# Splitting the last partitions of wo's tail into two small loads, and a section entry signalled by GpSimd

## The chip, the cores and the metric

The kernel runs on one core of a Trainium2 chip. The metric is the device time of one execution in microseconds (us); lower is better. Each time is a median of several runs; beside them one execution was taken by the profiler.

## The reference

A decode step mixes two branches by a gate. Branch A is attention over a cache (4 batches, 32 heads, 4096 keys of 128 floats); branch B is a feed-forward block with a gated GELU. All is float32.

```python
q = (x @ wq)                        # x: 4 x 1 x 512, wq: 512 x 4096, then 32 heads of 128
scores = einsum("bhqd,bhkd->bhqk", q, k_cache) * 128 ** -0.5
o = einsum("bhqk,bhkd->bhqd", softmax(scores), v_cache)
a = o.reshape(B, Sq, H * Dh) @ wo   # wo: 4096 x 512
b = (gelu(x @ w_gate) * (x @ w_up)) @ w_down
g = sigmoid((x * gate_w).sum(-1))
out = g * a + (1 - g) * b
```

The two caches are 268 MB each (4 x 32 x 4096 x 128 floats); wq and wo have 8.4 MB each and the three matrices of branch B 3.7 MB each. Each byte is read once.

## The kernel before, in words

The kernel is written as a list of steps. Each step names its engine, what it reads and what it writes, and a small planner (`Plan`) works out the waits: every lane (an engine, or a named lane for loads) has a semaphore, and a step waits for the lanes whose earlier steps it depends on. All loads are issued by SyncE (SP) through one helper, `load` (L251), and so stand in one queue in the order in which they are issued.

The work goes through 32 turns, one for each group of four heads and each batch. In a turn the keys of four heads come as one load of 8.4 MB (128 partitions x 16,384 floats), VectorE multiplies them by the query and sums (L377, L383), softmax follows on VectorE and ScalarE, and TensorE multiplies the weights with the values, another load of 8.4 MB (L409). All this works in one SBUF tensor, `big`, in which places are given out by hand.

Ahead of the turns stands an opening: the loads of wq, x, the first keys and the gate's weights. They are issued inside a critical section (`tc.tile_critical`, L585), whose entry and exit are signalled by one engine, by default SP. The other engines wait for its exit at a barrier (L588).

Behind the last turn come the loads of w_down (`load_d`) and of wo in two halves (`load_w`, L272). Half 0 comes in two loads. Half 1 comes in six: its 16 rows of 512 floats a partition are cut at 0, 4, 8, 11, 13 and 15, and each piece has a lane of its own, in this order f0, f1, g, v, y, w. The rows have `e` as their number; `DM` is 512, `P` is 128 and `E` is 16. For each row `e` of half 1, `project` (L478) makes four matmuls into `acc` from 32 columns of the attention's result and the row; `attended` (L469) says which places it reads, so a row waits for the lane that its piece came by. Row 15 is the last to come. Then VectorE copies `acc` to `res` (L578), and SP stores it (L579). At the end GpSimd clears the semaphores.

```python
    WO_END = ((0, E // 2, E), (0, 4, 8, 11, 13, 15, E))
```

Of the kernel before, what the change touches and what calls it, by code (L numbers as in the profile page):

```python
# [132 lines left out]
def tile_gated_mix(tc: tile.TileContext, x, kc, vc, wq, wo, w_gate, w_up, w_down, gate_w, out):  # L133
    nc = tc.nc
    P = 128
    B, H, S, D = kc.shape
    DM = x.shape[2]
# [15 lines left out]
    E = HW * D // P  # L153
# [12 lines left out]
    def sb(pool, name, shape):  # L166
        sizes[name] = math.prod(shape[1:])
        return pool(name, [P] + list(shape[1:]), F32).ap()[:shape[0]]
# [35 lines left out]
    q = sb(ps, "q", [P, B, D])  # L204
# [7 lines left out]
    W1, ES = TW, TW + TW // 2  # L212
    XS, U0, QD, FU, FT, OXA = VA - 2 * DM, VA - 4 * DM, VA - DM, VA + 2 * KC * F, ES + 2 * E * 32, ES + 2 * E * 32 + DM

    def place(a, n):
        return big[:, a:a + n]

    def z(a, n):
        return ("big", a, a + n)
# [4 lines left out]
    xTf = xT.rearrange("p c j b k -> p c (j b k)")  # L224
    selv = sel.rearrange("p j t m -> p j (t m)")
    x_sb = place(XS, DM)[:B]
    u = place(U0, 2 * DM).rearrange("p (s n) -> p s n", s=2)
    qd = place(QD, D)
    fu = place(FU, 2 * DM).rearrange("p (s n) -> p s n", s=2)
    OX = place(OXA, E * GW * HT * D // E)[:B * HT].rearrange("q (e g h k) -> q e g h k", e=E, g=GW, h=HT)  # L230
# [19 lines left out]
    def load(dst, src, writes, lane):  # L250
        return add("sp", lambda: nc.sync.dma_start(dst, src), (), writes, lane=lane, unit=16)  # L251
# [20 lines left out]
    def load_w(w):  # L272
        src = wo[w * HW * D:(w + 1) * HW * D].rearrange("(p e) n -> p (e n)", e=E)
        for n, (e0, e1) in enumerate(zip(WO_END[w], WO_END[w][1:])):
            a, m = (W0, W1)[w] + e0 * DM, (e1 - e0) * DM
            load(place(a, m), src[:, e0 * DM:e1 * DM], [z(a, m)], (("q", "x"), ("f0", "f1", "g", "v", "y", "w"))[w][n])

    load(place(Q0, KC * H * D), wq.rearrange("(p c) n -> p (c n)", c=KC), [z(Q0, KC * H * D)], "q")
    load(x_sb, x.rearrange("b s d -> (b s) d"), [z(XS, DM)], "x")
# [188 lines left out]

    def attended(w, e):  # L469
        a, m = ES + w * E * 32 + e * 32, (W0, W1)[w] + e * DM  # L470
        return place(a, 32), place(m, DM), [z(a, 32), z(m, DM)]

    def project_wide(s, w, reads):
        n = next(wide_rest)
# [49 lines left out]
    for i in range(NT):  # L524
        g, b = divmod(i, B)
# [30 lines left out]
    plan.turn = None  # L556
    load_d()
    load_w(0)
    load_w(1)
    expand(0)  # L560
    pv(NT - 1)
# [11 lines left out]
    for e in range(E):  # L573
        project_wide(*attended(0, e))
    fold()
    for e in range(E):
        project(*attended(1, e), False, e == E - 1)
# [4 lines left out]
        assert lane in ("sp", "out") or plan.knew[plan.steps[-1]][lane] == len(row_) - 1, lane  # L582
    plan.close()
    issued = nc.alloc_semaphore("issued")
    with tc.tile_critical(no_gpsimd_drain=True):  # L585
        plan.play(plan.steps[:opening])
    tc.close()
    tc.compile()  # L588
# [32 lines left out]
```

## Time and profile before

| What | Value |
|---|---|
| time, median of 3 runs | 1309.91 us (1309.84 to 1310.15) |
| time of the profiled execution | 1309.79 us |
| its span, first to last instruction | 1308.5 us |
| HBM read | 564.67 MB, 432 GB/s over the span |
| VectorE busy | 1153.3 us (88%) |
| TensorE matmul busy | 357.9 us (27%) |
| ScalarE busy | 86.9 us (7%) |
| GpSimd busy | 0.7 us |
| granted TensorE clock, mean | 0.636 |

The time is a little longer than the span, which runs from the first to the last instruction. The busy shares are means over the whole span. DMA engines aren't among the engines of the table; the profile gives their busy share as a mean over the core's 16.

### The profile page before, as it was taken

How to read it: one execution, taken by the hardware profiler on the slowest of the kernel's cores; microseconds unless marked ns; L12 is line 12 of the kernel's file. 1: busy time of each engine (PE TensorE's matmuls, PEld its weight loads, DVE VectorE, ACT ScalarE, POOL GpSimd, SP SyncE). 2: the span in 40 equal slices, each digit the busy share in tenths (PEclk: the TensorE clock that was granted, in tenths of full speed). 3: DMA queues.
4: the chain of work that ended last, by engine and by line, in shares of the span. 5: the costliest groups of instructions: out<-in, count | busy, mean ns of one | idle time of the engine just before them, and what ended most of it. 6: DMA issues, size and time to landing. Idle time of an engine off the chain costs nothing.

```text
span 1308.5 us, 6298 instructions
## 1 busy us (share of the span) xinstructions
PE 357.9 (27%) x2584; PEld 104.8 (8%) x2584; DVE 1153.3 (88%) x295; ACT 86.9 (7%) x289; POOL 0.7 (0%) x6
## 2 busy tenths in 40 slices
PE   2402333212332211322321123321123222122327
PEld 0200001000010000100000000100001000000003
DVE  1899999999899998989989898998989899898991
ACT  0000000000000000000000000000000000000001
POOL 0000000000000000000000000000000000000000
PEclk9656666556676656666655666655566665666668
DMA  9999999999999999999999999999999999999998
GB/s 417 417 447 427 437 439 427 439 431 441 425 441 425 443 427 439 439 429 439 431 441 425 441 425 443 427 439 439 429 441 429 441 425 441 425 443 429 435 431 364
DMA packets 11126, 564.82 MB, mean 432 GB/s; under 512 B 1368, under 2 KB 1384, under 8 KB 1900
## 3 DMA queue, kind: packets, MB, share of 16 engines
q1 hardware_dynamic: 11116, 564.68, 99.7%
q8 instruction: 7, 0.11, 0.0%
q14 instruction: 3, 0.02, 0.0%
HBM read 564.67 MB, written 0.01 MB: 432 GB/s over the span
## 4 chain that ended last, share of the span: by engine, by line
DMA 72%; DVE 26%; PE 1%; issue 1%; SPq 0%; ACT 0%; DVEq 0%
DMA big<-in_A_k_cache 66%; DVE sc L383 13%; DVE big L377 12%; DMA big<-in_A_wo 2%; DMA big<-in_B_w_up 2%; DMA big<-in_A_x 2%; PE po L312 1%; PE q L494 0%; SPq L251 0%; PE acc L481 0%; DVE hT L513 0%; DVE xT L303 0%; DVE m L388 0%; DVE big L511 0%; DVE big L508 0%
## 5 line engine op out<-in xcount | busy, mean ns | idle before, releaser
L377 DVE TENSOR_TENSOR big<-big,qb 128x4096 f32<-128x4096 f32 x64 | 556.0, 8687 | 87.7 <-DMA big<-in_A_k_cache 87.7
L383 DVE TENSOR_REDUCE sc<-big 128x32 f32<-128x4096 f32 x64 | 555.9, 8686 | 2.3
L409 PE MATMUL po<-big,PM 128*32 128x512 f32 x2048 | 296.1, 743 | 899.6 <-DMA big<-in_A_v_cache 899.6
L409 PEld LDWEIGHTS po<-big,PM 128*32 128x32 f32 x2048 | 72.7, 133 | 1116.6 <-DMA big<-in_A_v_cache 824.0
L395 ACT ACTIVATE PM<-sc,nb 32x128 f32<-32x128 f32 x128 | 67.2, 525 | 476.7 <-DVE nb L390 429.7
L417 ACT ACTIVATE o<-po 128x512 f32<-128x512 f32 x16 | 9.6, 597 | 449.8 <-PE po L409 449.8
L395 ACT ACTIVATION_READ_ACCUMULATOR PM<-sc,nb 32x1 f32 x128 | 26.1, 204 | 0.0
L367 ACT ACTIVATE qb<-q 128x512 f32<-128x512 f32 x8 | 4.8, 597 | 246.0 <-PE q L365 246.0
L426 PE MATMUL sm<-o,sel 128*16 128x128 f32 x128 | 15.4, 273 | 5.1 <-ACT o L417 5.1
L303 DVE COPY xT<-sg 128x128 f32<-128x128 f32 x4 | 0.9, 283 | 17.1 <-PE sg L298 17.1
L459 DVE TENSOR_TENSOR tm<-oT,gmask 128x256 f32<-128x256 f32 x2 | 0.8, 424 | 16.2 <-PE oT L453 16.2
L494 PE MATMUL q<-big,xT 128*32 128x448 f32 x64 | 10.5, 823 | 9.5 <-DMA big<-in_B_w_gate 4.9
L426 PEld LDWEIGHTS sm<-o,sel 128*16 128x16 f32 x128 | 11.7, 97 | 12.8 <-ACT o L417 11.4
L365 PE MATMUL q<-QM,hc 128*128 128x512 f32 x16 | 9.5, 678 | 4.2 <-DVE hc L361 4.2
L388 DVE TENSOR_REDUCE m<-sc 128x1 f32<-128x128 f32 x32 | 9.2, 286 | 1.1
L578 DVE COPY res<-acc 128x128 f32<-128x128 f32 x1 | 0.3, 291 | 10.1 <-PE acc L481 10.1
L312 PE MATMUL po<-big,xT 128*32 128x512 f32 x64 | 8.5, 692 | 1.0 <-DVE xT L303 1.0
L389 DVE STREAM_TRANSPOSE mt<-m 128x32 f32<-128x32 f32 x32 | 6.8, 211 | 1.1
L329 DVE TENSOR_TENSOR big<-po,amask 128x512 f32<-128x512 f32 x2 | 1.3, 686 | 7.3 <-PE po L312 7.3
L390 DVE TENSOR_REDUCE nb<-mt 128x1 f32<-128x32 f32 x32 | 6.0, 186 | 1.1
L298 PE MATMUL sg<-ident,big 4*128 4x4 f32 x4 | 0.6, 254 | 23.0 <-DMA big<-in_A_x 23.0
L481 PE MATMUL acc<-big 128*32 128x128 f32 x128 | 4.6, 276 | 1.8 <-DMA big<-in_A_wo 1.8
(62 smaller groups left out, 62.9 us busy)
## 6 DMA issues: line engine op xcount, KB each, us to landing
big<-in_A_wo SPq DMA_DIRECT2D x2, 2048.0 KB, 22.9
big<-in_B_w_gate SPq DMA_DIRECT2D x1, 3584.0 KB, 17.7
big<-in_B_w_up SPq DMA_DIRECT2D x1, 3584.0 KB, 26.9
big<-in_B_w_down SPq DMA_DIRECT2D x1, 3584.0 KB, 18.4
big<-in_A_wo SPq DMA_DIRECT2D x2, 1024.0 KB, 25.6
big<-in_A_wo SPq DMA_DIRECT2D x2, 512.0 KB, 29.2
big<-in_A_wo SPq DMA_DIRECT2D x1, 768.0 KB, 28.0
big<-in_A_k_cache SPq DMA_DIRECT2D x32, 29.7
```

The lines of the kernel that those rows point to most:

```text
L312: last = T.matmul(PO[s][32 * j:32 * j + 32].rearrange("p j d -> p (j d)"), xTf[:, c, :32], w[:, n0:n0 + HB * D], start=c == 0, stop=c == K ...
L365: pe(lambda: T.matmul(q.rearrange("p b d -> p (b d)"), HC.rearrange("p h k -> p (h k)"), QM.rearrange("p b d -> p (b d)"), start=True, sto ...
L377: dve(lambda: V.tensor_tensor(k, k, QB[:, b:b + 1, :].to_broadcast([P, r1 - r0, D]), op=OP.mult), m + t("qb"), m)
L383: dve(lambda: V.tensor_reduce(SC[i % 2][:, r0:r1], k, axis=AX.X, op=OP.add), [z(KA(i) + r0 * D, (r1 - r0) * D)], [(f"sc{i % 2}", r0, r1)])
L388: dve(lambda: V.tensor_reduce(M1[n], SC[n], axis=AX.X, op=OP.max), t(f"sc{n}"), t(f"m1{n}"))
L389: dve(lambda: V.transpose(MT, M1[n].to_broadcast([P, PH])), t(f"m1{n}"), t("mt"))
L390: dve(lambda: V.tensor_reduce(NB[n], MT, axis=AX.X, op=OP.max, negate=True), t("mt"), t(f"nb{n}"))
L395: last = A.activation(PM[:, PZ:].rearrange("p (c m) -> p c m", m=32)[s, :, h:RJ * HT:HT], SC[n][s, :].rearrange("p (c j) -> p c j", j=RJ), ...
L409: last = T.matmul(PO[n][32 * c:32 * c + 32].rearrange("p j d -> p (j d)"), PM[:, m0:m0 + 32], place(VAT(i) + j * N, N), start=b == 0 and j ...
L417: act(lambda: A.activation(O[n], PO[n], AF.Copy), t(f"po{n}"), t(f"o{n}"))
L426: T.matmul(sm[:B * HT, :D], selv[:, j, m0:m0 + B * HT], O[n][:, j, :], start=(n, j) == (0, 0), stop=(n, j) == (N - 1, RJ - 1))
L494: last = T.matmul(q.rearrange("p b d -> p (b d)")[32 * j:32 * j + 32, :FG], xTf[:, c, :32], place((F0, F1)[s] + c * F + j * FG, FG), start ...
```

## The change

There are two parts. First, for rows 11 to 15 of wo's half 1 (the loads v, y and w), the loads take only partitions 0 to 111. Partitions 112 to 127 of these five rows come in two loads of eight partitions each, with 2,560 floats (10,240 B) a partition, issued ahead of v, on new lanes e and h. Rows 11 to 15 read these places too, so TensorE waits for both ahead of row 11. Second, the critical section of the opening is entered and left on GpSimd's signal instead of SP's: SP loses an instruction that signals and keeps the wait, and GpSimd gets them.

```diff
+    UP = 11
...
         for n, (e0, e1) in enumerate(zip(WO_END[w], WO_END[w][1:])):
             a, m = (W0, W1)[w] + e0 * DM, (e1 - e0) * DM
-            load(place(a, m), src[:, e0 * DM:e1 * DM], [z(a, m)], (("q", "x"), ("f0", "f1", "g", "v", "y", "w"))[w][n])
+            if (w, e0) == (1, UP):
+                for p, lane in ((112, "e"), (120, "h")):
+                    load(place(a, (E - UP) * DM)[p:p + 8], src[p:p + 8, UP * DM:], [("upper", p, p + 8)], lane)
+            p = 112 if w == 1 and e0 >= UP else P
+            load(place(a, m)[:p], src[:p, e0 * DM:e1 * DM], [z(a, m)], (("q", "x"), ("f0", "f1", "g", "v", "y", "w"))[w][n])
...
-        return place(a, 32), place(m, DM), [z(a, 32), z(m, DM)]
+        return place(a, 32), place(m, DM), [z(a, 32), z(m, DM)] + ([("upper", 112, P)] if w == 1 and e >= UP else [])
...
-    with tc.tile_critical(no_gpsimd_drain=True):
+    with tc.tile_critical(sync_engine=mybir.EngineType.Pool, no_gpsimd_drain=True):
         plan.play(plan.steps[:opening])
```

## The prediction

> **What bounds the kernel now.** I read the page first, then the DMA share over long stretches, then the chain of waits and the timeline at the two ends.
>
> ```profile
> span 1308.5 us, 6298 instructions
> q1 hardware_dynamic: 11116, 564.68, 99.7%
> q8 instruction: 7, 0.11, 0.0%
> q14 instruction: 3, 0.02, 0.0%
> DMA 72%; DVE 26%; PE 1%; issue 1%; SPq 0%; ACT 0%; DVEq 0%
> ```
> ```profile
> 60.00:600.00 540.00, 133.74 (x924) 36.17 (x924) 501.60 (x121) 36.03 (x123) 0.00 (x0) 0.62 1.00 435
> 600.00:1264.00 664.00, 175.16 (x1200) 48.10 (x1204) 610.16 (x132) 43.58 (x149) 0.00 (x0) 0.62 1.00 434
> ```
>
> The second fence is the table by stage; its last two columns are the DMA share and GB/s. From 60 to 1264 us the sixteen DMA engines are busy for all of the time at 435 GB/s. The chain's 26% for DVE is therefore an accident of how it is followed (a load's issue waits for DVE), since the queue behind that issue never runs dry. The kernel is a stream of 564.68 MB. Its end can move in only three ways: the stream's first packet starts at another time, its last bytes land at another time, or the work behind the last landing changes. The change touches the first two. The price of a byte on one engine is 435/16 = 27.2 GB/s, so a row of 10,240 B (five of wo's rows of 512 floats) takes 0.38 us, one of 4,096 B 0.15 us, one of 2,048 B 0.075 us.
>
> The end, by the chain of waits and then by the timeline:
>
> ```profile
> 1275.61 29.56 DMA big<-in_A_wo
> 1305.21 1.06 PE acc L481 x24
> 1306.30 0.29 DVE res L578
> ```
> ```profile
> 1302.69 0.86 PE L481 MATMUL acc<-big 128*32 128x128 f32 x24 [0.76 <-DMA big<-in_A_wo]
> 1303.97 0.64 PE L481 MATMUL acc<-big 128*32 128x128 f32 x16 [0.42 <-DMA big<-in_A_wo]
> 1305.21 1.02 PE L481 MATMUL acc<-big 128*32 128x128 f32 x24 [0.60 <-DMA big<-in_A_wo]
> 1305.81 0.16 PEld L481 LDWEIGHTS acc<-big 128*32 128x32 f32 x8 [0.22 <-DMA big<-in_A_wo]
> 1306.62 0.67 SPq L579 DMA_DIRECT2D out<-res  x1
> ```
>
> PE starts at 1303.97 on rows 11 and 12 (the load named v), at 1305.21 on rows 13 and 14 (y), and at 1305.81 on row 15 (w). The 24 matmuls from 1305.21 take 1.02 us, although 24 in a row take 0.86 (the first line), because the last eight wait for w. So w's landing sets the end, and 1305.81 + 0.42 is the end of PE. The y landing has 1305.81 + 0.42 - (1305.21 + 0.86) = 0.16 us of slack.
>
> When does w land, and why so late? The table by stage again, near the end:
>
> ```profile
> 1303.00:1303.75 0.75, 0.56 (x22) 0.28 (x12) 0.00 (x0) 0.00 (x0) 0.00 (x0) 1.00 1.03 402
> 1303.75:1304.00 0.25, 0.03 (x4) 0.03 (x5) 0.00 (x0) 0.00 (x0) 0.00 (x0) 1.00 0.63 254
> 1304.00:1304.25 0.25, 0.25 (x12) 0.25 (x16) 0.00 (x0) 0.00 (x0) 0.00 (x0) 1.00 0.60 238
> 1304.25:1304.50 0.25, 0.25 (x16) 0.10 (x4) 0.00 (x0) 0.00 (x0) 0.00 (x0) 1.00 0.41 164
> 1304.50:1304.75 0.25, 0.12 (x5) 0.00 (x0) 0.00 (x0) 0.00 (x0) 0.00 (x0) 1.00 0.42 164
> 1304.75:1305.00 0.25, 0.00 (x0) 0.00 (x0) 0.00 (x0) 0.00 (x0) 0.00 (x0) 1.00 0.40 156
> 1305.00:1305.25 0.25, 0.04 (x4) 0.04 (x6) 0.00 (x0) 0.00 (x0) 0.00 (x0) 1.00 0.26 98
> 1305.25:1305.50 0.25, 0.25 (x12) 0.25 (x16) 0.00 (x0) 0.00 (x0) 0.00 (x0) 1.00 0.05 16
> ```
>
> Multiply the share by 16: all engines work until 1303.75, then 10, 10, 7, 7, 6, 4 and 1. Every engine carries the same bytes, yet about six stop before 1304, about three more before 1304.5, and about six go on to 1305.0-1305.4. What the engines do not share evenly is the ten instruction packets of q8 and q14 (first fence): seven of 0.11 / 7 = 0.016 MB, three of 0.02 / 3, some half of that. One of them, by the DMA view of 1292.5 to 1292.7 us:
>
> ```profile
> q8 instruction: 1, 0.02, 27.7%
> ```
>
> 0.277 x 16 x 0.2 us = 0.89 us on one engine. The stream never pauses, so what such a packet takes is never won back. My reading: the late six each met one q8 packet, the three in the middle one q14 packet. Work moved from the late engines to the early ones brings the end forward; the unused area above is (0.37 + 0.40 + 0.59 + 0.58 + 0.60 + 0.74 + 0.95) x 0.25 x 16 = 17 engine-us, so at most 17/16 = 1.06 us is there to gain.
>
> **The loads of rows 11 to 15.** Before, each engine carries 8 partitions of the three loads v, y, w. After, these have 112 partitions, 7 an engine if sixteen still share them evenly, and partitions 112 to 127 come in two loads of eight rows of 10,240 B, issued ahead of v. How does a load of few rows spread? The x load has four rows of 2,048 B and lands in four partitions. Two windows of 30 ns show its packets:
>
> ```profile
> DMA packets 5, 0.01 MB, mean 205 GB/s; under 512 B 2, under 2 KB 2, under 8 KB 5
> q1 hardware_dynamic: 5, 0.01, 56.2%
> DMA packets 3, 0.00 MB, mean 69 GB/s; under 512 B 2, under 2 KB 2, under 8 KB 3
> ```
>
> Three packets of 2 to 8 KB start within 30 ns, and one 0.17 us later. 0.562 x 16 x 30 = 270 ns of packet time for the three and two tiny ones, so some 85 ns each: they overlap, so they are on different engines, one row each, and lie in neighbouring partitions without slowing one another. So I take a load of eight rows as one row on each of eight engines, both loads on the same eight, call these the low eight, and the others the high eight. The Trainium skill (DMA: Bandwidth & Descriptors, section "Why a DMA increments its semaphore by 16 and not by 1") says that the number of engines is the largest one up to 16 that divides the rows, and that on the queues of SP the lowest-numbered are used; which eight, no view of before shows.
>
> Against before, at w's landing: a high engine has one row less, -0.38 us; a low engine has two more and one less, +0.38. At y's landing: high -2 x 0.15 = -0.30, low 0.76 - 0.30 = +0.46. At v: high -0.15, low +0.61.
>
> If the six late engines are all high, w's last landing goes from 1305.81 to 1305.43 for PE. The latest low engine is then one that stops at 1304.75 or so before and at 1305.13 after, against 1305.4 - 0.38 = 1305.0 for the high: the two sides end about together, and I allow 0.1 us there. For y PE starts at 1304.91 and would be done with 24 matmuls at 1305.77; w gives 1305.43 + 0.42 = 1305.85 and still sets the end. **-0.38 us.** Where the late engines lie can't be read before, and I take the high eight: the two classes of lateness go by queue (six by q8, three by q14), no engine shows two, so these packets have fixed homes, and a queue with its homes in one half is the simplest such pattern. That is a choice, not a reading.
>
> PE gets two more waits ahead of row 11, for the two small loads. They stand ahead of v in the same queue, and PE sat idle 0.42 us before 1303.97 on v alone, then 0.60 before 1305.21: that hides them, and even v's +0.61 on the early engines only fills what they had to spare. SP issues two loads more:
>
> ```profile
> 1275.13 0.43 SPq L251
> big<-in_A_wo SPq DMA_DIRECT2D x1, 256.0 KB, 29.7
> ```
>
> Two times 0.43 us delays w's issue by 0.9, and behind these on SP is only the output, at 1306.62. The w load lands 29.7 us after its issue, so a queue of nearly 29 us covers it; without that cover it would cost 0.9. Sixteen packets more, at 0.01 us of gaps each pair: nothing.
>
> **The entry.** The chain of waits at the start:
>
> ```profile
> 0.67 0.05 issue
> 0.72 0.02 SPq L585
> 0.74 0.07 issue
> 0.80 0.03 SPq L588
> 0.84 0.12 issue
> 0.96 0.40 SPq L251
> 1.42 21.40 DMA big<-in_A_x
> ```
> ```profile
> 0.34 0.10 POOL L610 MEMSET const-uint8-127<- 128x1 uint8 x1
> ```
>
> SP now signals to itself (L585) and then waits for it (L588), from 0.72 to 0.80; then comes the first load. After, GpSimd signals and SP only waits. GpSimd is done with its memsets at 0.44 and leaves the opening barrier about when SP does. If its signal is there when SP arrives, the load starts 0.08 us earlier; if it lags by a signal's flight, the gain is none or below: bounds +0.05 (half an issue gap of 0.12) and -0.08, and I take -0.06, nearer the row that goes away. The whole stream shifts with it. At the section's exit GpSimd's signal reaches the engines perhaps 0.1 us later; SP's next load waits for PE's projection and PE for x, which lands at 1.42 + 21.40, so nothing follows from it.
>
> **Sum.** The profiled execution took 1309.79 us (1308.5 of span and 1.29 around it); the median of the runs is 0.12 above it. 1309.79 - 0.38 - 0.06 = 1309.35, in terms of the median 1309.5 us: 0.03% faster, far inside the 0.2% (2.6 us) that a measurement of this kernel can tell from no change.
>
> **The rivals.**
> - *The late engines carry the small loads.* If the last engine of all is one of the low eight, its end moves by +0.38: PE starts row 15 at 1306.19, and the time is 1309.91 + 0.38 - 0.06 = 1310.2, slower than before. It decides as soon as the very last engine is low; if only an earlier one of the six is low (they stop 0.1 to 0.4 before the last), the end moves by 0 to +0.3, and the time lies between 1309.9 and 1310.2. For it: no view places them. Chance 0.26.
> - *The change doesn't do what it says.* If the small loads spread over all sixteen, or one on each half, every engine carries 8 rows as before, and only the entry is left: 1309.85. The packets of x speak against the first, nothing against the second. Chance 0.10. [...]
> - *An instruction packet more.* SP's program grows by two loads and the fetches shift; one more q8 packet on a late engine costs some 0.9 us: 1310.4 at best, with the gain of 0.38 taken off. Ten in 1308 us speak against it. Chance 0.06.
> - *112 partitions go slower than 128.* If seven rows an engine, no longer in step with eight partitions, took twice as long, that is 7 x 0.38 = 2.7 us more: 1312.1. The neighbours of the x load speak against it. Chance 0.02.
>
> **How the numbers follow.** The forecast has 0.55, the four rivals 0.44, and 0.01 is left for what I don't see. Forecast and first two rivals span 1309.35 to 1310.2; with the entry's bounds and the 0.3 us between the runs of before the range is 1309.2 to 1310.3. Faster than 1307.3 nothing here reaches (the whole unused area is 1.06 us): 0.01. Slower than 1312.5: the last rival's worst, 0.02. Within: 0.97.
>
> **What would show it.** Right: in the timeline SP's first load starts near 0.90; the share of DMA falls from full to nothing in a shorter stretch than the 1.75 us of before; PE starts row 15 about 0.38 earlier relative to the first load. Wrong: the staircase is as long or longer, with its last engines later (first rival), unchanged (second), or the landings of v, y, w are spaced wider than 1.24 and 0.60 us for every engine (fourth). A time outside 1309.2 to 1310.3 would say that something moved which is not in this list.

## The result, and the profile after

The changed kernel takes 1313.31 us (median of 11 runs, 1312.69 to 1313.67) against 1309.90 before: a ratio of 1.0024, 95% interval 1.0016 to 1.0033. It is slower by 3.4 us, where 0.4 us faster was forecast. Its profiled execution took 1313.05 us.

The start, by the chain of waits of the changed kernel (start, us, what):

```profile
0.61 0.02 POOLq L616
0.63 0.06 issue
0.69 0.02 POOLq L591
0.72 0.02 issue
0.73 0.03 SPq L594
0.77 0.12 issue
0.89 0.41 SPq L253
```

GpSimd signals at 0.69 and SP stops waiting at 0.73; the first load is issued at 0.89 in place of 0.96. That is the -0.07 which was forecast as -0.06.

The end, by the timeline of TensorE (PE):

```profile
1300.72 1.08 PE L487 MATMUL acc<-big 128*32 128x128 f32 x32 [0.28 <-DMA big<-in_A_wo]
1304.37 0.86 PE L487 MATMUL acc<-big 128*32 128x128 f32 x24 [2.57 <-DMA big<-in_A_wo]
1307.14 2.36 PE L487 MATMUL acc<-big 128*32 128x128 f32 x40 [1.90 <-DMA big<-in_A_wo]
1307.98 1.07 PEld L487 LDWEIGHTS acc<-big 128*32 128x32 f32 x24 [0.21 <-DMA big<-in_A_wo]
```

Rows 4 to 7 (the 32 matmuls) start at 1300.72, a tenth earlier than before. From there on all is late: row 8 starts at 1304.37 in place of 1302.69, row 11 at 1307.14 in place of 1303.97, row 13 at 1307.98 in place of 1305.21. SP's issues did not delay it: by the DMA view the load w (224 KB) landed 31.8 us after its issue, and the last issue of wo's ends at 1277.9. Why the bytes came late stands in the table by stage (the last three columns are PE's granted clock, DMA share and GB/s; a packet counts in full where it starts, so a share can pass 1), first before, then after:

```profile
1300.00:1302.00 2.00, 1.93 (x68) 1.45 (x56) 0.00 (x0) 0.00 (x0) 0.00 (x0) 1.00 1.02 422
1302.00:1304.00 2.00, 0.89 (x28) 0.62 (x29) 0.00 (x0) 0.00 (x0) 0.00 (x0) 1.00 0.95 382
1306.00:1306.50 0.50, 0.23 (x8) 0.00 (x0) 0.20 (x1) 0.00 (x0) 0.00 (x0) 1.00 0.00 0
```
```profile
1300.50:1301.00 0.50, 0.28 (x12) 0.28 (x16) 0.00 (x0) 0.00 (x0) 0.00 (x0) 1.00 1.41 438
1301.00:1301.50 0.50, 0.50 (x28) 0.50 (x20) 0.00 (x0) 0.00 (x0) 0.00 (x0) 1.00 0.92 160
1302.00:1304.00 2.00, 0.00 (x0) 0.00 (x0) 0.00 (x0) 0.00 (x0) 0.00 (x0) 1.00 0.99 223
1305.00:1306.00 1.00, 0.23 (x11) 0.00 (x0) 0.00 (x0) 0.00 (x0) 0.00 (x0) 1.00 0.95 250
1307.00:1307.50 0.50, 0.36 (x8) 0.39 (x12) 0.00 (x0) 0.00 (x0) 0.00 (x0) 0.50 0.29 111
1308.00:1308.50 0.50, 0.50 (x17) 0.49 (x16) 0.00 (x0) 0.00 (x0) 0.00 (x0) 0.50 0.00 0
```

All engines stay busy (0.99, 0.95) but move half the bytes: 223 to 250 GB/s instead of 382 to 422. The fall is sudden, from 438 to 160 GB/s at 1301, when the small loads and the first load of 112 partitions are under way (the 438 counts in full the rows of 10,240 B that start there). Single packets show the same: a row of the load g (6,144 B, one of 128 partitions) takes 0.234 us up to 1300, and from 1301 to 1303.5 every one of them takes 0.40 to 0.61. Had the loads piled up on a few engines, these would be busy and the others idle; here every engine is busy and slow.

The table shows a second loss. PE's granted clock is 0.50 from 1307 on, where before it was 1.00 until PE was done. The 24 matmuls from 1307.98 end with PE at 1309.50 (1307.14 + 2.36): 1.52 us, against 0.86 at full clock. At full clock w, landing at 1308.46, would have ended them at 1308.46 + 0.04 + 0.42 = 1308.92. So of the 3.27 us by which PE ends later (1306.23, that is 1305.21 + 1.02, to 1309.50), 0.58 are the clock and 2.69 the late landing, with the entry's gain already taken off.

### The profile page after: what moved, and what is told of

Read it like the earlier page. It is cut to its first block, busy times and chain, and to the rows that moved or that the text cites. A ratio compares the mean times of both kernels' runs of the same rounds, so it can differ in the third digit from the quotient of the medians.

```text
span 1311.7 us, 6303 instructions
## 1 busy us (share of the span) xinstructions
PE 356.3 (27%) x2584; PEld 105.7 (8%) x2584; DVE 1153.3 (88%) x295; ACT 86.9 (7%) x289; POOL 0.7 (0%) x6
## 3 DMA queue, kind: packets, MB, share of 16 engines
q1 hardware_dynamic: 11100, 564.68, 99.6%
## 4 chain that ended last, share of the span: by engine, by line
DMA 72%; DVE 26%; PE 1%; issue 1%; SPq 0%; ACT 0%; DVEq 0%; POOLq 0%
DMA big<-in_A_k_cache 66%; DVE sc L389 13%; DVE big L383 12%; DMA big<-in_A_wo 2%; DMA big<-in_B_w_up 2%; DMA big<-in_A_x 2%; PE po L318 1%; PE q L500 0%; PE acc L487 0%; SPq L253 0%; DVE hT L519 0%; DVE m L394 0%; DVE xT L309 0%; DVE big L517 0%; DVE big L516 0%
## 5 line engine op out<-in xcount | busy, mean ns | idle before, releaser
L415 PE MATMUL po<-big,PM 128*32 128x512 f32 x2048 | 292.9, 736 | 902.8 <-DMA big<-in_A_v_cache 902.8
```

What stands on the lines that cost most here:

```text
L415: last = T.matmul(PO[n][32 * c:32 * c + 32].rearrange("p j d -> p (j d)"), PM[:, m0:m0 + 32], place(VAT(i) + j * N, N), start=b == 0 and j ...
```

## Experiments: which part

Each time is a median beside the kernel before on the same chip, which took 1309.82 to 1309.88 us throughout.

**Entry only.**

```diff
-    with tc.tile_critical(no_gpsimd_drain=True):
+    with tc.tile_critical(sync_engine=mybir.EngineType.Pool, no_gpsimd_drain=True):
```

> Only the entry is signalled by GpSimd; the loads are as before. My step says -0.06 us: 1309.85, and SP's first load at 0.89 us of the span, as it stands after the whole change. If the entry carried part of the loss, the time would be above 1310.5.

Measured: 1309.96 us, ratio 1.000 (0.999 to 1.001). Its chain starts as that of the changed kernel does (first load at 0.89), so the 0.07 us are there at the start and too small for the runs to show. The entry carries none of the loss.

**Split loads only**, the changed kernel with the old entry.

> Only the loads of rows 11 to 15 are split; SP signals the entry. If the loads carry the whole loss: 1313.4 (0.07 above the whole change). First rival (only more bytes on late engines, at the usual price): at most 1310.3.

Measured: 1313.43 us, ratio 1.0027 (1.0017 to 1.0036). The loads carry all of it, and far above the 1310.3 that more bytes on late engines could give at the usual price.

**Small loads only.**

```diff
+            if (w, e0) == (1, 11):
+                for p, lane in ((112, "e"), (120, "h")):
+                    for a2, m2, c0 in ((VA + TW - 2 * DM, 2 * DM, 11 * DM), (VA - DM, DM, 13 * DM)):
+                        load(place(a2, m2)[p:p + 8], src[p:p + 8, c0:c0 + m2], ..., lane)
             load(place(a, m), src[:, e0 * DM:e1 * DM], [z(a, m)], ...)
```

> The loads v, y, w keep 128 partitions; ahead of v stand four loads of eight rows (partitions 112 to 119 and 120 to 127, 4,096 B and 2,048 B a row) into places that nothing reads, 12 KB more on each of eight engines. At the usual price 12,288 B / 27.2 = 0.45 us: 1310.4 at most. If the small loads are what slows all engines: 1 us more or above, 1311 to 1312, and the lines of the load g stretched as in the changed kernel.

Measured: 1311.23 us, ratio 1.001 (1.000 to 1.002): +1.35, three times the price of its bytes. In its trace w lands 1.2 us later than before (1306.97 for 1305.77); the rest is PE's half clock. The table by stage:

```profile
1300.00:1301.00 1.00, 0.28 (x12) 0.28 (x16) 0.00 (x0) 0.00 (x0) 0.00 (x0) 1.00 0.97 395
1301.00:1302.00 1.00, 0.81 (x32) 0.54 (x20) 0.00 (x0) 0.00 (x0) 0.00 (x0) 1.00 1.09 295
1302.00:1303.00 1.00, 0.00 (x0) 0.00 (x0) 0.00 (x0) 0.00 (x0) 0.00 (x0) 1.00 0.97 270
1303.00:1304.00 1.00, 0.37 (x16) 0.38 (x19) 0.00 (x0) 0.00 (x0) 0.00 (x0) 1.00 1.02 373
```

The rate falls while the small loads run (270) and comes back behind them (373), with v, y and w at 128 partitions. From 1301 to 1303 all 28 rows of g take 0.29 to 0.53 us in place of 0.234, so the small loads slow every engine that still carries g.

**112 partitions only.**

```diff
-            load(place(a, m), src[:, e0 * DM:e1 * DM], [z(a, m)], ...)
+            p = 112 if w == 1 and e0 >= 11 else P
+            load(place(a, m)[:p], src[:p, e0 * DM:e1 * DM], [z(a, m)], ...)
```

> The loads v, y, w take 112 partitions and the small loads are left out, so partitions 112 to 127 of rows 11 to 15 hold old values. At the usual price one row less an engine: -0.38 us, 1309.5. If loads of 112 partitions are what slows the engines (240 GB/s, as seen in the changed kernel, in place of 435): 1.15 MB take 4.8 us in place of 3.0 for 128 partitions, +1.8 and some 0.5 more at the end if TensorE's clock falls before its last matmuls: 1311.7 to 1312.2.

Measured: 1311.88 us, ratio 1.0016 (1.0007 to 1.0026): +2.0, although an eighth of the bytes of these rows isn't moved.

```profile
1300.00:1301.00 1.00, 0.06 (x4) 0.00 (x0) 0.00 (x0) 0.00 (x0) 0.00 (x0) 1.00 1.02 424
1302.00:1303.00 1.00, 0.08 (x4) 0.00 (x0) 0.00 (x0) 0.00 (x0) 0.00 (x0) 1.00 1.08 236
1303.00:1304.00 1.00, 0.00 (x0) 0.00 (x0) 0.00 (x0) 0.00 (x0) 0.00 (x0) 1.00 1.00 240
```

236 and 240 GB/s with busy engines, as in the changed kernel. Both parts slow the stream by themselves: 1.35 + 2.0 = 3.35, against 3.55 together. (The sum is rough, as the half clock lies in each.)

## Experiments: reads or writes

No view shows which engine writes which partition. I assumed that an engine takes neighbouring rows of a load: with 128 partitions eight rows of wo into eight neighbouring partitions, with 112 seven, so that most eights would be shared by two engines; in the small loads eight engines would share one. But row and partition have the same number, so the collision could be in HBM (theory S) or in SBUF (theory D). Four kernels pair them in all ways. All of half 1 comes in pairs of loads of 64 rows, four rows an engine. "Near" takes rows or partitions 0 to 63, then 64 to 127, so that (by the assumption) two engines share an eight; "far" takes the even ones, then the odd ones, so that each engine stays in its own eight. S and D in the slices below are one or the other; the lines that make a row wait for both loads of its pair are left out:

```diff
-            load(place(a, m), src[:, e0 * DM:e1 * DM], [z(a, m)], ...)
+                for h in range(2):
+                    load(place(a, m)[D], src[S, e0 * DM:e1 * DM], ..., lane)   # h*64:h*64+64 or h::2
```

**Rows near, partitions near.**

> All of wo's half 1 (4.2 MB, 9.6 us at 435 GB/s) in pairs of loads of 64 rows, rows 0 to 63 and 64 to 127, into the partitions of the same numbers: 4 rows an engine, so two engines work within the same eight neighbouring rows in HBM and the same eight partitions in SBUF. Both theories (S: reads of neighbouring rows collide in HBM; D: writes into neighbouring partitions collide in SBUF) expect it slow: at half the rate +9.6 us, 1319.5. If 64 rows or more loads cost nothing and neither holds: 1310.

**Rows far, partitions far.**

> The same pairs of loads, but even rows into even partitions, then odd rows into odd ones: each engine keeps to its own eight rows and eight partitions, as with 128. Both theories expect no loss: 1310. If it is the number of rows or of loads that costs: 1313 or more.

**Rows far, partitions near.**

> Even rows, then odd rows, into partitions 0 to 63, then 64 to 127 (rows land in other partitions than the reference has them). HBM side as with 128, SBUF side shared by two engines. S: 1310. D: 1319.5.

**Rows near, partitions far.**

> Rows 0 to 63, then 64 to 127, into even partitions, then odd ones (rows land in other partitions than the reference has them). HBM side shared by two engines, SBUF side as with 128. S: 1319.5. D: 1310.

| HBM rows | SBUF partitions | median, us | ratio (95%) |
|---|---|---|---|
| near | near | 1318.10 | 1.0061 (1.0037 to 1.0084) |
| far | far | 1309.89 | 1.0000 (0.9989 to 1.0012) |
| far | near | 1319.49 | 1.0074 (1.0044 to 1.0103) |
| near | far | 1309.83 | 1.0000 (0.9988 to 1.0011) |

The table by stage of each in the same stretch, in the order of the table:

```profile
1300.00:1302.00 2.00, 0.63 (x12) 0.16 (x8) 0.00 (x0) 0.60 (x1) 0.00 (x0) 1.00 0.98 221
```
```profile
1300.00:1302.00 2.00, 1.54 (x51) 1.00 (x40) 0.00 (x0) 0.00 (x0) 0.00 (x0) 1.00 0.99 407
```
```profile
1300.00:1302.00 2.00, 2.00 (x12) 0.20 (x4) 0.00 (x0) 0.00 (x0) 0.00 (x0) 0.58 1.02 225
```
```profile
1300.00:1302.00 2.00, 1.05 (x32) 0.81 (x32) 0.00 (x0) 0.00 (x0) 0.00 (x0) 1.00 1.01 416
```

The partitions decide alone: 221 and 225 GB/s into 64 neighbouring ones, 407 and 416 into every second one, whatever the rows. S has fallen; D stands in so far as the SBUF side decides. That it is two engines in one eight that collide is a reading; any grouping of the partitions in which 64 neighbouring ones belong to half as many groups as 64 alternate ones would give the same four times. That the loads of 112 partitions and of eight rows are slow for this same reason is inferred: these kernels have neither. That loads have 64 rows, or that there are twelve in place of six, costs nothing that can be measured. A rule of the Trainium skill (DMA: Bandwidth & Descriptors, section "Rules for kernel authors") advises against splitting a transfer into halves of the partitions, because they serialize over the same engines; here such halves cost 8 to 10 us for 4.2 MB, and halves of every second partition nothing, so it is not the splitting but which partitions a load takes. The same page of the Trainium skill (section "Specifications") lists eight partitions an engine as a convention; here every load has four an engine, and the two kernels that spread them lose nothing.

## Experiments: what an eight takes

**One more load behind the others.** 262 KB in eight rows of 32,768 B, which nothing uses; TensorE's last row waits for it. D says which partitions:

```diff
     spread(1)
+    load(place(0, E * DM)[D], wo[...][112:120], [z(0, E * DM)], "e")     # four rows: 112:116
```

Into partitions 112 to 119:

> Behind all loads of before stands one more, of eight rows of 32,768 B (262 KB, nothing uses them), into partitions 112 to 119; TensorE's last row waits for it. It runs while the other engines finish. If eight neighbouring partitions together take no more than one engine's 27.2 GB/s: 9.6 us, from 1303.9 on, PE about 7.7 us later and 0.5 more with its clock at half: 1318. If sixteen together share twice that: 4.8 us, 1313 to 1313.5. If 32 share four times that: 2.4 us, 1311. If nothing is shared and only an engine leaving its own partitions counts, no figure is given by the runs so far.

Into 0, 8 to 56:

> The same load of eight rows into partitions 0, 8, 16 to 56: one row for each of the eight engines, each in the eight partitions that it fills in loads of 128. 1.2 us an engine at the full rate; the latest of these engines may be among the last of all: 1310.2 to 1311.6 with the clock. Both readings of the collision (shared eights, or engines outside their own) expect this.

Into 64, 72 to 120:

> The same load into partitions 64, 72, 80 to 120: one engine to each eight, but none in its own. If sharing is what costs, as with partitions 0 to 56, 1310.2 to 1311.6, apart from the half microsecond in which the owners still write there. If an engine outside its own eight is slow by itself: clearly above, 1313 or more.

Four rows into 112 to 115:

> Four rows of 32,768 B (131 KB) into partitions 112 to 115, on four engines: the form of the x load with longer rows. My reading of x in the prediction (neighbouring partitions don't slow one another) expects 1.2 us an engine, 1310.2 to 1311.6. If eight neighbouring partitions share 27.2 GB/s: 4.8 us, 1313 to 1313.5.

Measured: 1314.98 us together (ratio 1.0038, 1.0023 to 1.0053), 1312.37 in their own eights (1.0020, 1.0010 to 1.0030), 1312.99 in others' (1.0022, 1.0012 to 1.0033), 1314.63 for four rows together (1.0034, 1.0019 to 1.0049). The order is as expected, but both spread loads are slower than the 1310.2 to 1311.6 that I gave, and the eight together faster than one engine's share would allow. The table by stage while the small load is on its way, eight together and then four together:

```profile
1305.00:1306.00 1.00, 0.00 (x0) 0.00 (x0) 0.00 (x0) 0.00 (x0) 0.00 (x0) 1.00 0.42 41
1306.00:1307.00 1.00, 0.00 (x0) 0.00 (x0) 0.00 (x0) 0.00 (x0) 0.00 (x0) 1.00 0.53 51
```
```profile
1305.00:1306.00 1.00, 0.19 (x8) 0.00 (x0) 0.00 (x0) 0.00 (x0) 0.00 (x0) 1.00 0.39 33
1306.00:1307.00 1.00, 0.00 (x0) 0.00 (x0) 0.00 (x0) 0.00 (x0) 0.00 (x0) 1.00 0.44 35
```

These GB/s are not the small load's: a packet counts where it starts, and its rows started before 1305 (all but one of the eight, which started at 1307.8). The DMA view of the four rows together from 1305 to 1306, and of the rows in their own eights from 1304.6 to 1305, shows what is counted:

```profile
DMA packets 17, 0.03 MB, mean 33 GB/s; under 512 B 2, under 2 KB 2, under 8 KB 17
q1 hardware_dynamic: 17, 0.03, 38.6%
```
```profile
DMA packets 33, 0.06 MB, mean 154 GB/s; under 512 B 5, under 2 KB 5, under 8 KB 33
q1 hardware_dynamic: 33, 0.06, 39.8%
```

All are under 8 KB, so they are rows of y and w. Beside the crowded rows they take 0.386 x 16 x 1 us / 15 = 0.41 us each, beside the spread ones 0.398 x 16 x 0.4 / 28 = 0.09. Up to six of them are slow at a time, although w goes to all 128 partitions and only four of these hold the crowded rows: the crowded rows slow the other engines too. They themselves take 3.2 to 4.8 us (four together) and 2.1 to 4.7 us (eight together) in the trace, where 27.2 GB/s would give 1.2. The four rows are the form of the x load, on which the prediction leaned, with rows 16 times as long: neighbouring partitions do slow one another. The x load's four rows took 84 ns each; that they were too short to show it is likely, and not tested.

The small load from its issue to its landing, by the chain of waits, eight together and then four together:

```profile
1287.82 22.69 DMA big<-in_A_wo
```
```profile
1287.92 22.44 DMA big<-in_A_wo
```

Twice the bytes into the same eight partitions take 0.25 us longer. So the eight is not one unit with one rate that its rows share.

**The same load alone.** The last four put it behind w's landing, so that it has the engines to itself:

```diff
+    load(place(0, E * DM)[D], wo[...][112:120], [z(0, E * DM), ("after", 0, 1)], "e")   # w writes ("after", 0, 1) too
```

> The load of eight rows of 32,768 B again, but SP issues it only after the load w has landed, so that no other load is in flight. Into partitions 112 to 119. Between 1305.8 and 1309.9 seven such rows took 39 GB/s in the run with others beside them; if the eight partitions take that much alone, 262 KB last 6.7 us, some 5.5 more than into partitions 0 to 56. If the others were what slowed it: as there.

> The same into partitions 0, 8 to 56, alone: 1.21 us for each packet (32,768 B at 27.2 GB/s), all eight alike. If packets still differ (1.2 to 2.3 us beside others), it isn't sharing that makes them differ.

> The same into partitions 64, 72 to 120, alone: one engine to each eight, none in its own. If only sharing costs: as into 0 to 56. If an engine outside its own eight is slow by itself: 1.8 us and more a packet, as the last one beside others had (1,784 ns).

> Two rows of 32,768 B into partitions 112 and 113, alone, on two engines. If eight neighbouring partitions take no more than about 39 GB/s: 65,536 B last 1.7 us, 1.7 a packet. If two engines go together at the full rate: 1.21.

Measured: 1316.44 us together (ratio 1.0051, 1.0028 to 1.0073), 1314.88 own (1.0037, 1.0022 to 1.0053), 1314.83 other (1.0038, 1.0018 to 1.0057), 1314.36 for two rows (1.0033, 1.0019 to 1.0047). The chain of waits of each has the load from its issue to its landing (start, us):

```profile
1305.82 6.37 DMA big<-in_A_wo
```
```profile
1305.91 4.85 DMA big<-in_A_wo
```
```profile
1305.90 4.80 DMA big<-in_A_wo
```
```profile
1305.96 4.29 DMA big<-in_A_wo
```

Own and other are alike, 4.85 and 4.80: which of the two sets of partitions it is makes no difference. Together it is 1.5 us more, not the 5.5 more that 39 GB/s would give. In the trace the eight rows together take 2.8 to 4.2 us each and 4.2 in all, 62 GB/s; the spread ones 1.5 to 2.6 each and 2.6 and 2.5 in all, 101 and 105 GB/s; the two rows 1.7 and 1.8, 36 GB/s. None comes to the 1.21 us that I had expected of the spread ones. The pause of all loads may be part of it: the first rows of wq, 65,536 B each, take 2.6 to 3.4 us, later ones 2.42.

One limit for an eight doesn't fit these numbers: 221 GB/s over eight eights is 28 for each where the whole stream goes into 64 neighbouring partitions, two rows alone in one eight got 36, and eight rows 62. Nor did eight rows in eight different eights run at the full rate, though there the pause may be the reason. So the runs show that rows in neighbouring partitions slow the stream, and not which partitions share a limit, nor what the limit is (a rate, or a queue that fills and holds up the engines behind it); both stay open.

## Why the prediction was wrong

- **What bounds the kernel** held: a stream of loads that ends the kernel, with PE's work behind w.
- **The entry** held in place and size: -0.07 for -0.06 at the first load; the runs can't tell it.
- **The step that failed** is the one on how a load of few rows spreads: from x's packets, "they overlap, so they are on different engines, one row each, and lie in neighbouring partitions without slowing one another", and from it the flat price of 27.2 GB/s for every row wherever it lands. Four rows of 32,768 B in neighbouring partitions took 3.2 to 4.8 us each, where that price gives 1.2, and slowed the rows of other engines beside them from 0.09 to 0.41 us. x told of rows of 2 KB and was used for rows five times as long, eight at a time.
- **The term that followed**, -0.38 for the loads of rows 11 to 15, was wrong in sign: w landed at 1308.46 in place of 1305.77, +2.69 (the entry's -0.07 within), because the sixteen engines together fell to 223 to 250 GB/s. The small loads and the loads of 112 partitions each do this by themselves (+1.35 and +2.0).
- **The fourth rival** (112 partitions go slower than 128, 1312.1, chance 0.02) had the right side and nearly the size, but for more than half of the loss only: by itself that part costs 2.0. It gave the wrong ground ("no longer in step"), left out the small loads (1.35), and its chance was set by the same reading of x.
- **The first rival** (late engines carry the small loads) was not settled: a price of 0.4 doesn't show beneath 2.7.
- **The second and third rivals** fell. In the trace the sixteen rows of 10,240 B are eight pairs, the second row of each starting within 3 ns of the end of the first, so eight engines carry two rows each, as the prediction took it. The instruction packets are seven and three, as before.
- **Small slips** without weight: the page has 16 packets fewer in q1 (11,100 for 11,116), not sixteen more; half of 0.12 is 0.06; the 1309.35 that the range starts from is the profiled execution's, 1309.5 in terms of the median.
- **Left out** was the clock: 0.6 us, because PE's last matmuls moved past the fall of the granted clock. A fall came between 1304 and 1308.5 us in each of these profiles (before: 1307.5, behind PE's last matmul), so this kernel, when its end moves by a few microseconds, loses about half of one more.
- **No change by more than 0.2%** had 0.97: the measured 0.26% lies just beyond it, with an interval that reaches 0.16%.

No variant beat the kernel before; the entry alone is as fast.

## What to carry to other kernels

If a stream of loads bounds a kernel, look at which partitions a load writes, not only at how many bytes each DMA engine carries: loads into 64 neighbouring partitions ran at half the rate, while loads into every second partition of 128 went at the full one. Balancing bytes between engines by splitting off some partitions makes loads that are no longer spread like one of 128, and here each of the two kinds slowed the stream, so its gain has to be set against that. And a reading from a transfer of a few KB says little of one that lasts.

## What the runs showed of the hardware that I had not expected

- In loads of 64 rows, 16 busy engines move 221 to 225 GB/s into neighbouring partitions and 407 to 416 into every second one, whichever rows of HBM they read.
- The slowdown reaches other engines: with v, y, w at 128 partitions, eight engines' small loads took the whole stream from 395 to 270 GB/s, and every row of g that ran beside them from 0.234 to 0.29 to 0.53 us. What passes it on from engine to engine, no run shows.
- Near the end of the changed kernel the granted TensorE clock fell from 1.00 to 0.50 (0.87 from 1306 to 1307 us, 0.50 after), and 24 matmuls took 1.52 us in place of 0.86. When it falls differs from run to run by a few microseconds (1304.1 in one profile, 1308.5 in another).
